# Holding back one weight load until a DMA transpose has landed: part one of the second fc1 block, after layer norm 2's transpose of token tile 1

## The chip, the cores and the metric

The kernel runs on 1 core of one Trainium2 chip. The metric is device time in microseconds (us). Runs are compared only with runs of the same state; where an execution was slow (over 1.5% above the fastest of the same kernel; all others count as fast) or at a lower clock, the text says so. The granted clock is the share of its full speed that TensorE was given. "Issue to landing" runs from the start of a DMA's issue until its data is reported to have arrived. "TensorE" is the matmul engine (PE in the profile; PEld is its weight load), "VectorE" is DVE, "ScalarE" is ACT, "GpSimd" is POOL, and "SyncE" is SP, which here only issues DMAs.

## The reference, cut to what matters

A diffusion-transformer block with B, N, D = 2, 256, 1152 and F = 4608, all in bf16. The part that matters here is the end of the attention half and the start of the MLP half:

```python
x = x + gate_a * (attention(...) @ wo)          # output projection
h2 = _layernorm(x) * (1 + scale_m) + shift_m    # layer norm 2 and its modulate
m = _gelu(h2 @ w_fc1) @ w_fc2                   # fc1: 1152 -> 4608, fc2 back
return x + gate_m * m
```

The 512 tokens are four tiles of 128. Tiles 0 and 1 are batch 0, tiles 2 and 3 are batch 1.

## The kernel before

All weight loads are issued in program order from SyncE. The one that is changed is the first part of the second fc1 block:

```python
    w_shift_m = load_rows("w_shift_m", wmod_v, S_SHIFT_M * D)     # each: 3 loads of 864 KB
    tc.add_manual_dep(first_load["w_shift_m"], transposed.ins.name, WAIT_FOR, ...)
    w_scale_m = load_rows("w_scale_m", wmod_v, S_SCALE_M * D)
    w_f1[0] = load_rows("w_f1_0", wfc1_v, 0)                      # fc1 columns 0 to 1151
    w_f1[1] = wide_tile("w_f1_1")                                 # fc1 columns 1152 to 2303
    for c0, c1 in ((0, PW), (PW, D)):                             # 864 KB, then 1728 KB; PW = 384
        load = nc.sync.dma_start(w_f1[1][:, :, c0:c1], wfc1_v[:, :, D + c0:D + c1])
    w_f1_1_rest = load.ins
    w_f1[2] = load_rows("w_f1_2", wfc1_v, 2 * D)
    # ... further loads
```

Layer norm 2 works by token tile. Each normalized tile is turned by a DMA transpose, issued from ScalarE, into `hT`, which fc1 reads:

```python
    def ln2_normalize(t, split, between):
        # ... rstd; xn2 = (x1 - mean) * rstd, on ScalarE and for odd t partly on VectorE
        nc.scalar.dma_start_transpose(hT[:, :, t * P:(t + 1) * P], xn2[:])

    def wo_group(t, i, pool_add):                 # output projection, 9 matmuls of 384 columns
        for k in range(KD):
            nc.tensor.matmul(pacc[:], aT[:, k, t * P:(t + 1) * P], w_o[:, k, c0:c1],
                             start=(k == 0), stop=(k == KD - 1))
        # ... tmp = pacc * gate_a;  x1 = tmp + x
```

fc1 starts with 12 column tiles (m) for batch 0 alone, then the same 12 for batch 1. Tiles 0 to 8 are in the first block, tiles 9 to 11 in the part that is moved. The second part waits for batch 1's modulate:

```python
    for b in range(B):
        # m = 0..5 stepped over k together, then m = 6..11 one after the other
        # ... f1_mm(..., m, k, b * N, (b + 1) * N, ...): 108 matmuls of 256 columns per batch
        if b == 0:
            mods = [ln2_modulate(1, k) for k in range(KD)]        # VectorE, needs tiles 2 and 3
            tc.add_manual_dep(w_f1_1_rest, mods[0].ins.name, WAIT_FOR, reason="transposes first")
    # ... m = 12..35 over all 512 tokens
```

Of the kernel before, what the change touches and what calls it, by code (L numbers as in the profile page):

```python
# [19 lines left out]
def kernel(  # L20
# [11 lines left out]
    nc = tc.nc  # L32
    B, N, D = x.shape
# [3 lines left out]
    P = 128  # L37
    T = B * N
    NT = T // P
    TPB = N // P  # L40
    KD = D // P
    KF = F // P
    PW = 384
# [6 lines left out]
    WAIT_FOR = mybir.DependencyInfo(mybir.DependencyClass.Sync, mybir.DependencyReason.DATA)  # L50
# [9 lines left out]
    def acc_tile(shape, name, dt=FP32):  # L60
        return psum.tile(shape, dt, name=name, tag="acc", bufs=6)
# [11 lines left out]
    wfc1_v = w_fc1.rearrange("(k p) n -> p k n", p=P)  # L73
# [4 lines left out]
    def wide_tile(name):  # L78
        return wide.tile([P, KD, D], BF16, name=name, tag="wide")
# [37 lines left out]
    def load_rows(name, view, col0):  # L117
        w = wide_tile(name)
        for r in range(0, KD, 3):
            load = nc.sync.dma_start(w[:, r:r + 3, :], view[:, r:r + 3, col0:col0 + D])  # L120
            first_load.setdefault(name, load.ins)
        return w
# [15 lines left out]
    w_f1 = [None] * 4  # L138
# [89 lines left out]
    def ln_exp_rsqrt(dst, var):  # L228
        nc.scalar.activation(dst, var, ACT.Ln, bias=eps_t[:], scale=1.0)
        nc.scalar.activation(dst, dst, ACT.Exp, scale=-0.5)  # L230
# [195 lines left out]
    hT = act.tile([P, KD, T], BF16, name="hT")  # L426
# [189 lines left out]
    w_scale_m = load_rows("w_scale_m", wmod_v, S_SCALE_M * D)  # L616
    w_f1[0] = load_rows("w_f1_0", wfc1_v, 0)
    w_f1[1] = wide_tile("w_f1_1")
    for c0, c1 in ((0, PW), (PW, D)):
        load = nc.sync.dma_start(w_f1[1][:, :, c0:c1], wfc1_v[:, :, D + c0:D + c1])  # L620
    w_f1_1_rest = load.ins
    w_f1[2] = load_rows("w_f1_2", wfc1_v, 2 * D)
    w_f1[3] = load_rows("w_f1_3", wfc1_v, 3 * D)
    w_gate_m = load_rows("w_gate_m", wmod_v, S_GATE_M * D)
# [31 lines left out]
    def ln2_modulate(b, k, eng="d"):  # L656
        h = hT[:, k, b * N:(b + 1) * N]
        if eng == "a":
            return nc.scalar.activation(
                h, h, ACT.Identity, bias=shift_m[:, k, b:b + 1], scale=scale_m[:, k, b:b + 1],  # L660
            )
        return nc.vector.tensor_scalar(
            h, h, scale_m[:, k, b:b + 1], shift_m[:, k, b:b + 1], op0=ALU.mult, op1=ALU.add,
        )

    def ln2_normalize(t, split, between):
        rstd = small.tile([P, 1], FP32, name="rstd", tag="rstd")
        ln_exp_rsqrt(rstd[:], mv2[:, t, 1:2])
        for k, eng in between:
            ln2_modulate(0, k, eng)  # L670
        nb = small.tile([P, 1], FP32, name="nb", tag="nb")
        nc.vector.tensor_scalar(nb[:], mv2[:, t, 0:1], rstd[:], -1.0, op0=ALU.mult, op1=ALU.mult)
        xn2 = work.tile([P, D], BF16, name="xn", tag="xn", bufs=4)
        cs = 5 * P if split else D
        if cs < D:
            nc.vector.tensor_scalar(
                xn2[:, cs:D], x1[:, t, cs:D], mv2[:, t, 0:1], rstd[:],
                op0=ALU.subtract, op1=ALU.mult,
            )
        nc.scalar.activation(xn2[:, 0:cs], x1[:, t, 0:cs], ACT.Identity, bias=nb[:], scale=rstd[:])  # L680
        nc.scalar.dma_start_transpose(hT[:, :, t * P:(t + 1) * P], xn2[:])

    stats2 = [small.tile([P, NPD, 6], FP32, name="stats2", tag="stats2") for _ in range(NT)]

# [18 lines left out]
    def ln2_stats(t, i):  # L703
        nc.vector.bn_stats(stats2[t][:, i, :], x1[:, t, i * PW:(i + 1) * PW])
        if i == NPD - 1:
            nc.vector.bn_aggr(mv2[:, t, :], stats2[t][:].rearrange("p a b -> p (a b)"))
            ln2_normalize(t, t % 2 == 1, BETWEEN.get(t, ()))
# [33 lines left out]
    def f1_mm(dst, m, k, c0, c1, start, **kw):  # L741
        ml = m % KD
        nc.tensor.matmul(  # L743
            dst, w_f1[m // KD][:, k, ml * P:(ml + 1) * P], hT[:, k, c0:c1],
            start=start, stop=(k == KD - 1), **kw,
        )
# [6 lines left out]
    for b in range(B):  # L753
        for stepped in (True, False):
            ms = range(0, MSPLIT // 2) if stepped else range(MSPLIT // 2, MSPLIT)
            accs = {m0: acc_tile([P, 2, N], "pacc") for m0 in ms[::2]} if stepped else {}
            steps = [(m, k) for k in range(KD) for m in ms] if stepped else [(m, k) for m in ms for k in range(KD)]
            for m, k in steps:
                m0 = m - m % 2
                if m0 not in accs:  # L760
                    accs[m0] = acc_tile([P, 2, N], "pacc")
                f1_mm(accs[m0][:, m - m0, :], m, k, b * N, (b + 1) * N, start=(k == 0 and m == m0), skip_group_check=True)
                if k == KD - 1 and m == m0 + 1:
                    nc.scalar.activation(  # L764
                        gT[:, m0:m0 + 2, b * N:(b + 1) * N], accs[m0][:], ACT.Gelu_apprx_tanh,
                    )
        if b == 0:
            mods = [ln2_modulate(1, k) for k in range(KD)]
            tc.add_manual_dep(w_f1_1_rest, mods[0].ins.name, WAIT_FOR, reason="transposes first")
    gate_m = None  # L770
    for m in range(MSPLIT, KF):
        pacc = acc_tile([P, T], "pacc")
# [81 lines left out]
```

## Time and profile before

| | before |
|---|---|
| time, median of 3 | 243.78 us (243.64 to 244.18) |
| span, mean granted TensorE clock | 241.8 us, 0.998 |
| TensorE busy | 235.4 us, 97% |
| the load to be moved: issued, issue to landing | 78.1 us, 17.0 us |
| transposes of tiles 0, 1, 3: issue to landing | 8.4, 3.2, 3.2 us (tile 2's landing is not in this profile) |

The page of the kernel before: the first lines give the span and each engine's busy time; the last is the chain of work that ended last, by engine.

```profile
span 241.8 us, 3979 instructions
PE 235.4 (97%) x1688; PEld 144.4 (60%) x1698; DVE 91.5 (38%) x193; ACT 59.9 (25%) x121; POOL 28.3 (12%) x47
...
PE 94%; issue 2%; ACT 2%; POOL 1%; DVE 0%; POOLq 0%; DVEq 0%; ACTq 0%
```

The same chain in order of time (start us, length us, what), at the place where the output projection (L690) gives way to fc1 (L743). TensorE goes from one to the other without a wait.

```profile
88.90 8.88 PE pacc L690 x54
97.78 23.80 PE pacc L743 x217
```

The timeline around that place (start us, length us, engine, line, operation; in brackets the idle time just before and what ended it). A line ending in "q" is the issuing of a DMA, not its transfer.

```profile
78.09 29.66 SPq L620 DMA_DIRECT2D w_f<-in_w_fc_dram  x2
...
87.33 1.45 ACTq L681 DMA_TRANSPOSE hT<-xn  x1
...
93.66 1.31 ACTq L681 DMA_TRANSPOSE hT<-xn  x1
...
96.48 0.24 DVE L706 BATCH_NORM_AGGREGATE mv<-stats 128x2 f32<-128x18 f32 x1
96.98 0.60 DVE L662 TENSOR_SCALAR hT<-hT,scale_m,shift_m 128x256 bf16<-128x256 bf16 x2 [0.26 <-DMA hT<-xn]
...
97.62 27.63 PE L743 MATMUL pacc<-hT,w_f 128*128 128x256 bf16 x233
...
107.00 2.40 DVE L662 TENSOR_SCALAR hT<-hT,scale_m,shift_m 128x256 bf16<-128x256 bf16 x9 [3.90 <-DMA hT<-xn]
```

The first modulate (L662) is ready 0.26 us after VectorE is, and the first fc1 matmul has no idle in front of it. The bracket on the last line is VectorE waiting for tile 3; TensorE does not wait there.

Issue to landing of the transposes (their line):

```profile
L681 ACTq DMA_TRANSPOSE hT<-xn x4: 1306/1382/1498, 87.3 to 103.7; - x4
DMA to landing us min/median/max: 3.2/3.2/8.4
```

The slow one is tile 0's: in a window that holds only its issue at 87.3 us the same view gives 8.4.

What SyncE's queue waits for (us in total, times, longest). The two parts share line L620.

```profile
SPq L620 <- DVE hT L662: 21.2, 1, 21.2
...
SPq L620 <- DMA w_f<-in_w_fc_dram: 7.9, 1, 7.9
```

### The profile page before, as it was taken

What the parts mean: (1) busy time and instruction counts of PE and PEld (TensorE: products, weight loads), DVE (VectorE), ACT (ScalarE), POOL (GpSimd) and SP (SyncE); (2) the same over time, 40 slices, a digit from 0 to 9 for tenths busy, and PEclk for the clock granted to TensorE, in tenths of its full rate; (3) what the DMA queues carried; (4) which work ended last, traced back from release to release, by engine and by line L of the source; (5) the groups of instructions that cost most, each with busy time, mean ns of one, the idle gap of its engine ahead of it and who ended that gap; (6) DMA issues with size and microseconds to landing.
All of it is one profiled execution on the core that took longest, in us unless ns stands there. A gap on an engine that the chain in (4) does not pass through costs nothing.

```text
span 241.8 us, 3979 instructions
## 1 busy us (share of the span) xinstructions
PE 235.4 (97%) x1688; PEld 144.4 (60%) x1698; DVE 91.5 (38%) x193; ACT 59.9 (25%) x121; POOL 28.3 (12%) x47
## 2 busy tenths in 40 slices
PE   8799999999999999999999999999999999999994
PEld 5585444465567566888844444444556665566674
DVE  3742442319325678830002999960010000000001
ACT  6633322307215032671422333222000000000000
POOL 2300000002300324100000000001121111111111
PEclk9999999999999999999999999999999999999999
DMA  6999999997579999239999999999200000000000
GB/s 188 327 317 310 378 366 393 389 391 247 147 263 398 387 377 159 49 59 361 391 391 391 340 327 284 274 327 284 98 16 16 20 16 16 19 18 19 27 23 16
DMA packets 48781, 53.29 MB, mean 220 GB/s; under 512 B 9587, under 2 KB 36475, under 8 KB 48763
## 3 DMA queue, kind: packets, MB, share of 16 engines
q1 hardware_dynamic: 41312, 50.14, 62.5%
q10 hardware_dynamic: 6939, 1.71, 4.7%
q0 software_dynamic: 512, 1.19, 1.5%
q8 instruction: 13, 0.21, 0.4%
q14 instruction: 5, 0.04, 0.0%
HBM read 50.14 MB, written 1.19 MB: 212 GB/s over the span
## 4 chain that ended last, share of the span: by engine, by line
PE 94%; issue 2%; ACT 2%; POOL 1%; DVE 0%; POOLq 0%; DVEq 0%; ACTq 0%
PE pacc L799 29%; PE pacc L743 29%; PE pacc L690 7%; PE pacc L599 7%; PE pq L521 7%; PE pk L280 5%; PE pk L309 2%; PE pa L639 2%; PE ps_s L556 2%; PE pn L416 2%; ACT sink L206 1%; PE pt L264 1%; PE pm L247 1%; PE pg L498 0%; ACT rstd L335 0%
## 5 line engine op out<-in xcount | busy, mean ns | idle before, releaser
L743 PE MATMUL pacc<-hT,w_f 128*128 128x256 bf16 (+1 forms) x427 | 70.3, 325 | 0.3
L799 PE MATMUL pacc<-w_f,gT 128*128 128x384 bf16 (+2 forms) x468 | 70.5, 314 | 0.0
L799 PEld LDWEIGHTS <-gT 128*128 128x128 bf16 x468 | 44.4, 98 | 26.2
L743 PEld LDWEIGHTS <-w_f 128*128 128x128 bf16 x432 | 42.2, 98 | 27.6
L805 DVE TENSOR_TENSOR tmp<-pacc,gate 128x384 f32<-128x384 f32 (+2 forms) x13 | 6.9, 527 | 65.6 <-PE pacc L799 57.2
L775 ACT ACTIVATE gT<-pacc 128x512 bf16<-128x512 f32 x24 | 14.3, 597 | 32.6 <-PE pacc L743 32.6
L469 DVE SCALAR_TENSOR_TENSOR part<-w_gate_m,s,part 128x1152 f32<-128x1152 bf16 x16 | 21.4, 1414 | 0.0
L807 POOL TENSOR_TENSOR o_sb<-tmp,x 128x384 bf16<-128x384 f32 (+1 forms) x12 | 11.7, 973 | 54.0 <-DVE tmp L805 54.0
L690 PE MATMUL pacc<-w_o,big 128*128 128x384 bf16 x108 | 17.9, 326 | 0.0
L521 PE MATMUL pq<-hT,w_q 128*128 128x512 bf16 x79 | 17.7, 379 | 0.1
L599 PE MATMUL pacc<-w_v,hT 128*128 128x384 bf16 x108 | 17.7, 326 | 0.0
L599 PEld LDWEIGHTS <-hT 128*128 128x128 bf16 x108 | 10.5, 98 | 7.1 <-issue 0.3
L690 PEld LDWEIGHTS <-big 128*128 128x128 bf16 x108 | 10.4, 98 | 7.2 <-issue 0.4
L521 PEld LDWEIGHTS <-w_q 128*128 128x128 bf16 x81 | 7.9, 98 | 9.4
L280 PE MATMUL pk<-big,w_k 128*128 128x256 bf16 (+1 forms) x70 | 13.1, 324 | 0.1
L696 POOL TENSOR_TENSOR x<-tmp,x_sb 128x384 f32<-128x384 f32 x8 | 7.3, 914 | 27.4 <-DVE tmp L695 27.4
L467 DVE TENSOR_SCALAR part<-w_gate_m,s 128x1152 f32<-128x1152 bf16 x2 | 1.6, 818 | 22.3 <-DMA w_gate_m<-in_w_mod_dram 22.3
L491 POOL DMA_DIRECT2D gates_dram<-nat_v x2 | 1.1, 536 | 67.7 <-DVE nat_v L489 67.7
L280 PEld LDWEIGHTS <-w_k 128*128 128x128 bf16 x72 | 6.7, 97 | 3.7 <-issue 0.3
L764 ACT ACTIVATE gT<-pacc 128x512 bf16<-128x512 f32 x12 | 6.5, 598 | 8.9 <-PE pacc L743 8.9
L512 POOL DMA_DIRECT2D gates_dram<-nat x4 | 2.3, 584 | 49.3 <-DVE nat L509 48.7
L695 DVE TENSOR_TENSOR tmp<-pacc,gate 128x384 f32<-128x384 f32 x12 | 6.6, 549 | 3.1 <-PE pacc L690 3.1
(102 smaller groups left out, 164.2 us busy)
## 6 DMA issues: line engine op xcount, KB each, us to landing
w_f<-in_w_fc_dram SPq DMA_DIRECT2D x12, 864.0 KB, 14.9
w_f<-in_w_fc_dram SPq DMA_DIRECT2D x3, 1728.0 KB, 7.9
w_f<-in_w_fc_dram SPq DMA_DIRECT2D x2, 2592.0 KB, 17.2
w_gate_a<-in_w_mod_dram SPq DMA_DIRECT2D x3, 864.0 KB, 11.9
w_v<-in_wqkv_dram SPq DMA_DIRECT2D x3, 864.0 KB, 13.8
w_o<-in_wo_dram SPq DMA_DIRECT2D x3, 864.0 KB, 14.0
w_shift_m<-in_w_mod_dram SPq DMA_DIRECT2D x3, 864.0 KB, 6.6
w_scale_m<-in_w_mod_dram SPq DMA_DIRECT2D x3, 864.0 KB, 12.1
```

The costliest lines, as they stand in the source:

```text
L280: nc.tensor.matmul(pk[m][:, c0:c1], w_k[:, k, m * P:(m + 1) * P], hT0[:, k, c0:c1], start=(k == 0 and c0 == 0), stop=(k == KD - 1), skip_g ...
L469: nc.vector.scalar_tensor_tensor(part[:, b, :], wg[:, k, :], s32[:, k, b:b + 1], part[:, b, :], op0=ALU.mult, op1=ALU.add,)
L521: nc.tensor.matmul(pq[m][:], w_q[:, k, m * P:(m + 1) * P], hT[:, k, :], start=(k == 0), stop=(k == KD - 1), skip_group_check=True,)
L599: nc.tensor.matmul(pacc[:], hT[:, k, t * P:(t + 1) * P], w_v[:, k, pnl * PW:(pnl + 1) * PW], start=(k == 0), stop=(k == KD - 1),)
L690: nc.tensor.matmul(pacc[:], aT[:, k, t * P:(t + 1) * P], w_o[:, k, c0:c1], start=(k == 0), stop=(k == KD - 1),)
L695: nc.vector.tensor_tensor(tmp[:], pacc[:], gate_a[:, b, c0:c1], op=ALU.mult)
L696: (nc.gpsimd if pool_add else nc.vector).tensor_tensor(x1[:, t, c0:c1], tmp[:], x_sb[:, t, c0:c1], op=ALU.add)
L743: nc.tensor.matmul(dst, w_f1[m // KD][:, k, ml * P:(ml + 1) * P], hT[:, k, c0:c1], start=start, stop=(k == KD - 1), **kw,)
L775: nc.scalar.activation(gT[:, m, :], pacc[:], ACT.Gelu_apprx_tanh)
L799: nc.tensor.matmul(pacc[:], gT[:, kk, t * P:(t + 1) * P], w_f2[j][:, r, c0 - n * PW:c0 - n * PW + cw], start=(kk == 0), stop=(kk == KF - 1),)
L805: nc.vector.tensor_tensor(tmp[:], pacc[:], gate_m[:, b, c0:c0 + cw], op=ALU.mult)
L807: (nc.vector if last else nc.gpsimd).tensor_tensor(o_sb[:], tmp[:], x1[:, t, c0:c0 + cw], op=ALU.add)
```

## The change

The intent is to keep the queue free for the transposes: before, 864 KB of weights that nobody needs yet stand in front of them. The order of instructions stays the same on every engine; one wait is added.

```diff
-    for c0, c1 in ((0, PW), (PW, D)):
-        load = nc.sync.dma_start(w_f1[1][:, :, c0:c1], wfc1_v[:, :, D + c0:D + c1])
-    w_f1_1_rest = load.ins
+    w_f1_1_parts = [
+        nc.sync.dma_start(w_f1[1][:, :, c0:c1], wfc1_v[:, :, D + c0:D + c1]).ins
+        for c0, c1 in ((0, PW), (PW, D))
+    ]
@@ ln2_normalize
-        nc.scalar.dma_start_transpose(hT[:, :, t * P:(t + 1) * P], xn2[:])
+        turned = nc.scalar.dma_start_transpose(hT[:, :, t * P:(t + 1) * P], xn2[:])
+        if t == TPB - 1:
+            tc.add_manual_dep(w_f1_1_parts[0], turned.ins.name, WAIT_FOR, reason="transposes first")
@@ after fc1's batch 0
-            tc.add_manual_dep(w_f1_1_rest, mods[0].ins.name, WAIT_FOR, reason="transposes first")
+            tc.add_manual_dep(w_f1_1_parts[1], mods[0].ins.name, WAIT_FOR, reason="transposes first")
```

TPB is 2, so the wait is on token tile 1.

## The prediction

> **What bounds the kernel.** TensorE. The head of the page gives it busy 235.4 of 241.8 us (97%); the chain of waits runs through it for 94%; granted clock 1.00. Where the change acts there is nothing to win back: in windows from 86 to 109 us TensorE is busy in all 23 of 23 us. In the timeline the last output-projection matmul ends at 97.78 us, the first fc1 matmul (L743) starts at 97.62, and the next 132 follow at 110 ns each without a gap.
>
> **What the change does.** No instruction is added, removed or reordered on any engine; only one wait differs. The 864 KB load of the first 384 columns of the second fc1 block, issued at 78.09 us and landing 17 us later (95.1) behind queued loads, is now issued after token tile 1's transpose has landed.
>
> *Gain.* The transposes are issued from ScalarE, the loads from SyncE; the Trainium skill, "DMA: Bandwidth & Descriptors", section "Issuing engines are not separate DMA queues", says that both run on the same 16 engines and interleave. The trace agrees: tile 0's transpose, issued at 87.33 us into a full queue, took 8.4 us to land (95.7), the other three 3.2. Without the 864 KB the weight stream ends about 2.5 us earlier (estimate: 0.88 MB at the 320 to 330 GB/s of 90 to 92 us), so tile 0 lands near 91 to 93.
>
> *Why it is worth nothing.* Batch 0's modulate (VectorE, L662) needs tile 1 too, which is issued at 93.66 us, when the loads are nearly done, and lands at 96.86. VectorE ends its statistics at 96.72 and starts the modulate at 96.98, idle 0.26 us. The first fc1 matmul can then start at 97.3; TensorE is free at 97.6. Gain on the critical path: 0, at most 0.1 us.
>
> *Cost.* The load starts at about 96.9 us. The 1728 KB part of that block took 7.1 us to land with a free queue; half should take about 5 (estimate), landing near 102. Its first reader is column tile 9 in batch 0, the 82nd fc1 matmul: 97.62 + 81 x 0.110 = 106.5 us. Slack 4.5 us. It may delay tile 2's transpose (issued 100.02) by up to 1.5 us, but batch 1's modulate waits for tile 3 (issued 103.69, landed 106.9), when the load is over; TensorE needs batch 1 only at 109.5 us. The second part still waits for that modulate (issued 107.4), so later loads keep their times. Cost 0.
>
> **Predicted time:** 243.8 us, 8 in 10 from 243.3 to 244.4; faster by over 2%: 0.01, within 2%: 0.98, slower by over 2%: 0.01.
>
> **What the profile should show.**
> 1. DMA issues: the slowest of the four transposes falls from 8.4 us to 3 to 6; the others stay at 3.2 (tile 2 perhaps 4 to 5).
> 2. SyncE's waits: a new one on the transpose, some 19 us (78 to 97); the wait on the modulate falls from 21.2 to about 10.
> 3. The first part lands in about 5 us instead of 17.
> 4. The hole in DMA traffic at 97 to 100 us fills; 89 to 92 us empties.
> 5. First fc1 matmul at 97.6 (±0.2), TensorE busy throughout 95 to 115, span 241.8 ± 0.4; the second modulate wait ends at 107.0 ± 0.3.
>
> **What would make it wrong.** The load, meeting the transposes, lands after 106.5 us (TensorE stalls before column tile 9), or delays tile 3's transpose by over 2 us (a stall at batch 1's first matmul). If tile 1's 3.2 us still contain contention, the modulate starts earlier, but TensorE's own work ends at 97.78 and caps the gain.

## The result, and the profile after

| | before | after |
|---|---|---|
| time, median of 6 runs each | 243.65 us (243.57 to 244.18) | 243.47 us (243.17 to 244.06) |
| span, clock | 241.8 us, 0.998 | 241.4 us, 1.000 |
| tile 0's transpose, issue to landing | 8.4 us | 5.1 us |
| the moved load, issue to landing | 17.0 us (from 78.1) | 5.0 us (from 96.5) |
| start of fc1 on the chain, to the end of the span | 97.78, 144.0 us | 97.40, 144.0 us |

The ratio is 0.999, with a 95% interval of 0.9975 to 1.0006: the same time. Here and below a ratio is the mean time of one kernel's fast runs over that of the other's of the same rounds, so it is not quite the ratio of the medians that are quoted.

The lines that answer to those of before. Line numbers have moved: the transposes are L682, the output projection L693, the modulate L663, fc1 L746; the load is still L620. The page of the kernel after:

```profile
span 241.4 us, 3978 instructions
PE 236.4 (98%) x1688; PEld 145.1 (60%) x1698; DVE 91.4 (38%) x193; ACT 59.9 (25%) x121; POOL 28.3 (12%) x47
...
PE 94%; issue 2%; ACT 2%; POOL 1%; DVE 0%; POOLq 0%; DVEq 0%; ACTq 0%
```

Its chain in order of time at the same place:

```profile
88.52 8.88 PE pacc L693 x54
97.40 23.80 PE pacc L746 x217
```

Its timeline:

```profile
86.95 1.26 ACTq L682 DMA_TRANSPOSE hT<-xn  x1
...
93.28 1.31 ACTq L682 DMA_TRANSPOSE hT<-xn  x1
...
96.09 0.24 DVE L709 BATCH_NORM_AGGREGATE mv<-stats 128x2 f32<-128x18 f32 x1
96.54 10.80 SPq L620 DMA_DIRECT2D w_f<-in_w_fc_dram  x2
96.59 0.60 DVE L663 TENSOR_SCALAR hT<-hT,scale_m,shift_m 128x256 bf16<-128x256 bf16 x2 [0.26 <-DMA hT<-xn]
...
97.23 28.06 PE L746 MATMUL pacc<-hT,w_f 128*128 128x256 bf16 x235
...
106.60 2.40 DVE L663 TENSOR_SCALAR hT<-hT,scale_m,shift_m 128x256 bf16<-128x256 bf16 x9 [3.89 <-DMA hT<-xn]
```

Its transposes, from issue to landing (without tile 2's landing):

```profile
L682 ACTq DMA_TRANSPOSE hT<-xn x4: 1259/1310/1335, 86.9 to 103.3; - x4
DMA to landing us min/median/max: 3.2/3.2/5.1
```

What its SyncE queue waits for:

```profile
SPq L620 <- DMA hT<-xn: 18.9, 1, 18.9
...
SPq L620 <- DVE hT L663: 10.2, 1, 10.2
```

The load was moved as intended, by 18 us, and tile 0's transpose lands 3.3 us sooner. Nothing on TensorE answers. VectorE waits the same 0.26 us for the batch 0 modulate. The 0.38 to 0.40 us by which the lines of TensorE, VectorE and ScalarE are earlier here is not due to the change: it is there already before 14 us in the chains (the same group of four x transposes starts at 13.38 us before and at 13.00 after). From the start of fc1 to the end both take 144.0 us.

### The profile page after: what moved, and what is told of

Its sections match the earlier page's. It is cut to its first block, busy times and chain, and to the rows that moved or that the text cites. A ratio compares the mean times of both kernels' runs of the same rounds, so it can differ in the third digit from the quotient of the medians.

```text
span 241.4 us, 3978 instructions
## 1 busy us (share of the span) xinstructions
PE 236.4 (98%) x1688; PEld 145.1 (60%) x1698; DVE 91.4 (38%) x193; ACT 59.9 (25%) x121; POOL 28.3 (12%) x47
## 4 chain that ended last, share of the span: by engine, by line
PE 94%; issue 2%; ACT 2%; POOL 1%; DVE 0%; POOLq 0%; DVEq 0%; ACTq 0%
PE pacc L802 29%; PE pacc L746 29%; PE pacc L693 7%; PE pacc L599 7%; PE pq L521 7%; PE pk L280 5%; PE pk L309 2%; PE pa L640 2%; PE ps_s L556 2%; PE pn L416 2%; ACT sink L206 1%; PE pt L264 1%; PE pm L247 1%; PE pg L498 0%; ACT rstd L335 0%
## 5 line engine op out<-in xcount | busy, mean ns | idle before, releaser
L746 PE MATMUL pacc<-hT,w_f 128*128 128x256 bf16 (+1 forms) x427 | 70.3, 325 | 0.3
L746 PEld LDWEIGHTS <-w_f 128*128 128x128 bf16 x432 | 42.2, 98 | 27.6
L693 PE MATMUL pacc<-w_o,big 128*128 128x384 bf16 x108 | 17.9, 326 | 0.0
L693 PEld LDWEIGHTS <-big 128*128 128x128 bf16 x108 | 10.4, 98 | 7.2 <-issue 0.4
L173 PE MATMUL pwarm<-zeros 128*128 128x256 f32 x18 | 7.4, 587 | 1.2 <-DVE eps_t L93 1.2
```

The source lines that it names most:

```text
L173: nc.tensor.matmul(dst[:, 0:T // 2], zeros32[:, 0:P], zeros32, start=True, stop=True)
L746: nc.tensor.matmul(dst, w_f1[m // KD][:, k, ml * P:(ml + 1) * P], hT[:, k, c0:c1], start=start, stop=(k == KD - 1), **kw,)
```

## The experiments

**Theory A (slack at both ends).** Batch 0's modulate needs tile 1 as well as tile 0, and tile 1 is issued so late that it lands in 3.2 us with or without the load in front. TensorE is also busy with the output projection until just then. At the other end the load has some 4 us to spare before column tile 9 reads it. **Rival B (cancelling).** The earlier tile 0 is a real small gain, which the later load pays back. **Rival C.** Loads and transposes in one another's way cost nothing here, wherever the load stands.

The times of "before" below are those of the kernel before in the same rounds (11 runs per call; median 243.94 in the first call, 243.96 in the second, 243.87 in the third).

### Both kernels again

No edit.

> The kernel before, unchanged, for a second profile of it. All theories: about 243.6 us. Asked of it: whether the landing of token tile 0's transpose (8.4 us in the first profile) and the start of the weight stream (the shift_m load at 67.1 us, 64.8 in the profile after) repeat. If 8.4 comes back near 8, the fall to 5.1 us is due to the change; if it comes back near 5 to 6, part of the fall is the start of the stream, which differs from run to run.

> The changed kernel, unchanged, timed in five rounds. Theory A (slack at both ends: the batch 0 modulate waits for tile 1, which lands fast in both kernels, and the load has some 4 us to spare): ratio 1.000, within 0.998 to 1.002. Rival B (a small gain from the earlier tile 0, paid back by the later load): also near 1, but then fc1 must start earlier against the end of the output projection and stall later, before column tile 9; A expects neither. Tile 0's transpose lands in about 5 us again, tiles 1 to 3 in 3.2.

> The changed kernel once more. One of its 12 timed executions so far took 245.71 us at a mean clock of 0.993, while 28 executions of the kernel before lay between 243.35 and 244.39. If the change brings such executions now and then (TensorE idling before fc1 and falling to half clock, as in the run with the wait on tile 0), about one in ten should show again; if it was a disturbance of that execution, all six should lie between 243.1 and 244.4 and the ratio at 0.998 to 1.001.

Measured. The kernel before, second profile (one run, so of unknown state): 243.39 us, tile 0 lands in 8.7 us, the moved load in 17.3. The kernel after, five rounds: median 243.49 us, ratio 0.9998 (0.9969 to 1.0026); tile 0 lands in 4.7, tile 1 in 3.2, the load in 4.8. Once more: median 243.78 us, ratio 0.9987 (0.9956 to 1.0018); tile 0 in 4.9, tile 1 in 3.2, the load in 5.0. From the start of fc1 on the chain to the end of the span all three take 144.0 us.

The stream of weights starts at different moments from run to run (the shift_m load was issued at 67.1 us in both profiles of before, at 64.8, 65.1 and 68.0 in those of after), but tile 0 took 4.7 to 5.1 in all three, so its fall from 8.4 or 8.7 belongs to the change.

One execution of the changed kernel took 245.71 us at a clock of 0.993. None of the next six did, and one of the 11 executions of the kernel before took 246.33 us at 0.993. Both kernels have such an execution now and then. A mean clock of 0.993 is what the profiles below show where TensorE ran at half clock for one spell of about 3.4 us (1.7 us of clock missing of some 247); no profile caught such an execution of these two kernels, so what sets it off in them is not shown.

### The load after tile 0 instead of tile 1

Against the kernel after:

```diff
-        if t == TPB - 1:
+        if t == 0:
```

> The load now waits for tile 0's transpose instead of tile 1's, so it is issued at about 92 us and its bytes meet tile 1's transpose (issued 93.3). Theory A has only 0.3 us of slack at the modulate, so whatever tile 1 loses goes straight into the time: if transposes wait until queued loads have drained (as tile 0's packets seem to in the traces), tile 1 starts near 96 and lands near 98.5, fc1 starts about 2 us late, 245.5 us (244.5 to 246). If the two queues share the DMA engines evenly, tile 1 loses about 0.6 to 1 us: 244.3. Rival C (contention of loads and transposes costs nothing wherever the load stands): 243.5, tile 1 lands in 3.2 us.

> The kernel with the wait on tile 0 once more: its executions lay between 243.27 and 248.15 us, and the profiled one was a slow one (tile 0 landed at 93.5 us, so the load was issued at the same moment as tile 1's transpose, which then took 6.0 us). Theory A with a race: where tile 0 lands in about 5 us, the load gets in front by 1 us or more and tile 1 lands late by 2 to 4 us (245 to 248 us, with or without half clock); where tile 1's transpose is issued first, it lands in 3.2 us and the time is 243.3. The spread should come back.

Measured. First: ratio 1.0029 (0.9995 to 1.0063); the four fast runs 243.27, 244.24, 245.23 and 246.10 us, two slow runs 247.71 and 248.15. Second: ratio 1.0034 (0.999 to 1.0078), median 244.83 us, all four runs fast (244.78 to 245.34). The second profile, a fast one, its timeline:

```profile
92.30 16.83 SPq L620 DMA_DIRECT2D w_f<-in_w_fc_dram  x2
...
93.67 2.00 ACTq L682 DMA_TRANSPOSE hT<-xn  x1
...
98.43 0.60 DVE L663 TENSOR_SCALAR hT<-hT,scale_m,shift_m 128x256 bf16<-128x256 bf16 x2 [1.70 <-DMA hT<-xn]
98.83 26.55 PE L746 MATMUL pacc<-hT,w_f 128*128 128x256 bf16 x228 [1.03 <-DVE hT L663]
```

The load is issued 1.4 us before tile 1's transpose, which now lands in 4.7 us instead of 3.2. The modulate starts 1.4 us late, and 1.0 us of this reaches TensorE as idle time. By medians the kernel is 0.96 us slower than before (244.83 against 243.87). The intervals of both ratios still include 1, so it is the trace, more than the time, that speaks against Rival C here; the run with more load, below, settles it. There are only 0.3 to 0.4 us of slack.

The first set's profile was of a slow execution (247.71 us), so its time is not compared, but its trace shows a worse meeting. The load was issued at 93.58 us, just after tile 1's transpose at 93.53, which still took 6.0 us to land; after TensorE's idle time the granted clock (third number from the end of the second line) is halved:

```profile
100.06 25.19 PE L746 MATMUL pacc<-hT,w_f 128*128 128x256 bf16 x214 [2.42 <-DVE hT L663]
...
101.00:102.00 1.00, 1.00 (x7) 0.71 (x5) 1.00 (x3) 1.00 (x2) 0.85 (x1) 0.50 0.00 0
```

The spread of the first set (its fast runs reach from no loss to over 2 us) did not come back within the second, where it had been expected to.

### The load after tile 2

Against the kernel after:

```diff
-        if t == TPB - 1:
+        if t == 2:
```

> The load waits for tile 2's transpose: issued at about 102.9 us (99.6 + 3.2), landing 5 us later at 107.9. Theory A puts the first reader, the 82nd fc1 matmul, at 106.3 us, so TensorE stalls about 1.6 us there, once, and the time is 245.1 us (244.4 to 246.0); nothing else moves. Rival C and a load that is not read so early: 243.5 us.

Measured: the four fast runs 246.51 to 249.45 us, ratio 1.0157 (1.0122 to 1.0192), and two slow runs of 250.4 and 250.6 us at a clock of 0.986. In the profile (span 245.4 us, fast) the load was issued at 103.7 us; the chain of work shows how long it took (start us, length us, what):

```profile
103.74 6.30 DMA w_f<-in_w_fc_dram
```

TensorE's timeline:

```profile
98.05 9.01 PE L746 MATMUL pacc<-hT,w_f 128*128 128x256 bf16 x81
110.09 15.13 PE L746 MATMUL pacc<-hT,w_f 128*128 128x256 bf16 x136 [3.03 <-DMA w_f<-in_w_fc_dram]
```

TensorE stops after exactly 81 fc1 matmuls, before column tile 9, as Theory A has it. The stall is 3.03 us, not 1.6. Most of the difference is the landing: the load met tile 3's transpose (issued 104.12) and took 1.3 us longer than the 5.0 us assumed, and that transpose took 6.6 us itself. The slack of the changed kernel is real but small: by the ratio, one token tile later costs 3.8 us. The stall is 3.03 us of it in the profile, whose clock was full; two of the four fast runs also had a lower clock (0.992 and 0.993).

### More load in front of the transposes, without and with the wait

Here the collision is made three times as large. Against the kernel before, the second part loses its wait (the next block takes it over):

```diff
-            tc.add_manual_dep(w_f1_1_rest, mods[0].ins.name, WAIT_FOR, reason="transposes first")
+            tc.add_manual_dep(first_load["w_f1_2"], mods[0].ins.name, WAIT_FOR, reason="transposes first")
```

> The kernel before, with the second part of the block (1728 KB) freed of its wait as well, so that both parts (2.65 MB) stand in the queue in front of the transposes of tiles 0 and 1; the next block's first load takes over the wait for batch 1's modulate, so later loads keep their place. Theory A: the queue drains some 4.5 us later than before (estimate from 1728 KB at about 390 GB/s), near 96, and tiles 0 and 1 land near 100 in place of 96.9; fc1 starts 3 us late and the time is 247 us (246 to 249; TensorE's idle can bring a spell at half clock, as in the run with the wait on tile 0). Rival C (contention costs nothing wherever it stands): 243.6.

Measured: 251.44 us median (250.45 to 253.56), ratio 1.0327 (1.0295 to 1.036). Tile 0's transpose took 13.5 us and landed at 101.0; tile 1's came last, 8.57 us after its issue. The chain and TensorE's timeline:

```profile
93.84 8.57 DMA hT<-xn
...
102.83 22.35 PE L743 MATMUL pacc<-hT,w_f 128*128 128x256 bf16 x188 [4.87 <-DVE hT L662]
```

The stall is 4.87 us, where 3 was expected, and after it the clock falls. The same run in windows of 1 or 2 us (window, its length, then busy us and number of instructions on PE, PEld, DVE, ACT, POOL; then the granted clock, the DMA share and GB/s):

```profile
102.00:103.00 1.00, 0.17 (x2) 0.25 (x3) 0.57 (x3) 0.57 (x2) 0.00 (x0) 1.00 0.00 0
103.00:104.00 1.00, 1.00 (x8) 0.76 (x7) 1.00 (x4) 1.00 (x4) 0.30 (x1) 0.62 0.00 0
104.00:106.00 2.00, 2.00 (x11) 1.45 (x10) 1.97 (x5) 1.25 (x2) 0.61 (x1) 0.50 0.00 0
106.00:108.00 2.00, 2.00 (x18) 1.64 (x16) 1.56 (x7) 1.10 (x3) 0.00 (x0) 0.84 0.79 147
108.00:110.00 2.00, 2.00 (x21) 1.79 (x19) 0.48 (x2) 0.92 (x1) 0.00 (x0) 1.00 0.00 0
```

After the stall TensorE does 11 matmuls in 2 us instead of 21, at a granted clock of 0.50. The Trainium skill, "TensorE: Matmul & The Clock Gate", Part 1, describes this: after an idle window of about 3.4 us the clock is halved until TensorE has again been busy for such a window. The trace agrees in size: 0.38 + 1.0 + 0.32 us of clock are missing in these windows, half of 3.4 us. The stall of 4.87 us and these 1.7 us make up the 6.5 us by which the profiled execution (250.45 us, clock 0.993) is longer than before. It was the fastest of the six; the other five had a clock of 0.984 to 0.986, as if they had about two such spells, but none of these was profiled.

Now with the changed kernel's wait on tile 1 for both parts. Against the kernel after:

```diff
-            tc.add_manual_dep(w_f1_1_parts[1], mods[0].ins.name, WAIT_FOR, reason="transposes first")
+            tc.add_manual_dep(first_load["w_f1_2"], mods[0].ins.name, WAIT_FOR, reason="transposes first")
```

The second part stands behind the first on SyncE's queue, so it waits for tile 1 too.

> The change's wait on tile 1's transpose for both parts, the counterpart of the run before. Theory A: tiles 0 and 1 land as in the changed kernel, fc1 starts on time; the two parts are moved at about 98 to 104.5 us and meet the transposes of tiles 2 and 3, which may make batch 1's modulate 1 to 1.5 us late, within its 2 us of slack. 243.6 us (243.2 to 244.6): the same wait is worth about 3 us here, because here it takes away a collision that reached tile 1.

Measured: 244.87 us median (244.50 to 245.20), ratio 1.0043 (1.0026 to 1.0059). So here the wait is worth 6.6 us (251.44 to 244.87), the lost clock included. It is 0.9 us slower than before, not equal to it, and TensorE's timeline shows where:

```profile
110.57 14.77 PE L746 MATMUL pacc<-hT,w_f 128*128 128x256 bf16 x121 [0.87 <-DVE hT L663]
```

Batch 1's modulate started at 110.16 us instead of 106.6. Tile 2's transpose (issued 99.84) took 9.2 us to land and tile 3's (issued 103.99) took 6.1. What the queues moved in stretches of 2 us (queue 1 carries SyncE's loads, queue 10 ScalarE's DMAs, here only the transposes; packets, MB, share of the 16 engines), at 100 to 102 us, 102 to 104 us and 104 to 106 us:

```profile
q1 hardware_dynamic: 701, 0.72, 109.2%
...
q1 hardware_dynamic: 487, 0.75, 106.5%
...
q1 hardware_dynamic: 407, 0.62, 84.9%
q10 hardware_dynamic: 424, 0.11, 24.2%
```

From 100 to 104 us queue 10 moved nothing, although tile 2's transpose had been handed over by 101.6 us. It gets going only after 104 us, and then the two queues move about as many packets each (407 and 424). A packet of the load is about 1.5 KB there and one of the transpose about 0.25 KB, so equal turns leave the transpose 0.11 MB of 0.73. The same shows in the run before, which had no wait, from 94 to 96 us:

```profile
q1 hardware_dynamic: 417, 0.62, 85.0%
q10 hardware_dynamic: 427, 0.11, 26.1%
```

### TensorE's own work as the only cap?

The prediction gave two reasons for a gain of 0: tile 1's landing and TensorE's own work. Here the second is taken away: six matmuls of the output projection are left out, in both kernels. Their outputs are wrong, which doesn't matter for the times.

```diff
-        for k in range(KD):
+        kd = KD - 2 if t == NT - 1 else KD
+        for k in range(kd):
...
-                start=(k == 0), stop=(k == KD - 1),
+                start=(k == 0), stop=(k == kd - 1),
```

> Wrong result on purpose: the kernel before with 6 of the output projection's matmuls of token tile 3 left out, so TensorE is free 0.98 us earlier (6 x 0.164). It asks whether TensorE's own work was the only cap on the gain. Theory A: the modulate still waits for tile 1 at 96.9 us, fc1 starts at about 97.3 instead of 97.6 to 97.8, so only 0.3 to 0.5 of the 0.98 us are won: 243.2 us, and TensorE idles some 0.5 us before fc1.

> Wrong result on purpose: the changed kernel with the same 6 matmuls left out. Theory A: the same time as the run before within 0.2 us (243.2), with the same idle before fc1, since tile 1 lands at the same time in both. Rival B (the earlier tile 0 is a real gain that TensorE's work hid, paid back elsewhere): fc1 starts earlier here than in the run before and the kernel is 0.3 to 0.6 us faster than it.

Measured: before with the cut 243.82 us (ratio to before 1.0001, 0.9981 to 1.0021), after with the cut 243.57 us (0.9993, 0.9976 to 1.0009). TensorE's timeline of the first:

```profile
97.34 27.84 PE L744 MATMUL pacc<-hT,w_f 128*128 128x256 bf16 x235 [0.67 <-DVE hT L662]
```

and of the second:

```profile
97.59 27.71 PE L747 MATMUL pacc<-hT,w_f 128*128 128x256 bf16 x234 [0.55 <-DVE hT L663]
```

With TensorE free 0.98 us earlier, both kernels idle 0.55 to 0.67 us in front of fc1, waiting for the same modulate. Tile 0's transpose took 8.8 us in one and 5.2 in the other; tile 1's took 3.3 and 3.2. The times differ by 0.25 us, less than the spread of either (about 0.6 to 1.2 us). Neither came down to the expected 243.2 us: what the cut itself should win (0.3 to 0.5 us) did not show in the time either. So the earlier tile 0 is worth nothing that shows even when TensorE could use it, and Rival B, which expected 0.3 to 0.6 us and an earlier fc1, gets no support. A gain of 0.1 or 0.2 us is beyond what these rounds resolve.

## Why the prediction was right

**The time** (243.8, range 243.3 to 244.4): measured 243.47 us against 243.65 before, ratio 0.999. No term of the sum was above 0.1 us, and none was found. The number alone says little: a gain of 0.3 us, as Rival B has it, would have fallen into the range as well. What carries the mechanism is the traces and the runs above.

**Gain of 0.** The mechanism held: tile 0 landed in 5.1 us instead of 8.4, at 92.0 us, in the predicted 91 to 93. Both caps held in the traces: VectorE waits for tile 1 for the same 0.26 us, and TensorE goes on to fc1 without a gap. Tile 1 landed in 3.2 us in all profiles of both kernels (3.3 in the second of before). Taking TensorE's cap away changed nothing between the two kernels. That the collision can cost time at all was shown by the runs that push it onto tile 1: about 1 us with the load after tile 0 (a stall of 1.03 us in the trace), 7.5 us with 2.65 MB in front (in its profile a stall of 4.87 us and 1.7 us of lost clock).

**Cost of 0.** The load landed in 5.0 us, at 101.5, and the first reader was the 82nd fc1 matmul: with the load after tile 2, TensorE stopped after exactly 81. At the pace of the chain, that reader comes at 97.4 + 81 x 0.110 = 106.3 us, so the slack was about 4.8 us against the 4.5 predicted. Tile 2's landing was recorded in neither profile (the "other three" of the prediction are two), so its delay, for which "up to 1.5" had been allowed, is not measured; tile 3 landed in 3.2 us, and batch 1's modulate waited for it as long as before (3.89 and 3.90 us).

**What the profile should show.** Points 1 to 4 came true: the slowest transpose, the waits on SyncE (18.9 and 10.2 us, against 19 and 10), the landing of 5 us, and the hole in DMA traffic at 97 to 100 us, which now carries 50, 280 and 358 GB/s; 89 to 92 us emptied for the loads and kept the rest of tile 0's transpose. Point 5 was right in what it was about, but its absolute times (97.6 and 107.0) came out 0.4 us early (97.23 and 106.60), because that execution started 0.38 us earlier. A time in a trace should be predicted relative to something before the change, such as the end of the output projection.

**What was too small.** Not the prediction, but three expectations took the meeting of loads and transposes too lightly: the stall after tile 2 (3.03 us, not 1.6), the freed second part (4.87 us, not 3, plus the halved clock), and both parts after tile 1 (0.9 us slower, not equal). In the last two, where both queues moved data, they moved equal numbers of packets and not of bytes, and the transpose has the small packets; before that, its queue moved nothing for a while (above). In the changed kernel the load had landed at 101.5 us, before tile 3's transpose was issued (103.30), and batch 1's modulate starts no later for it; so the prediction was not hurt.

## What to carry to other kernels

A long wait in a trace is worth something only if it is the last of the waits that its reader needs: tile 0's 8.4 us looked costly, but the modulate also needs tile 1, which was issued 6 us later and landed in its shortest time anyway. Before moving a load, write down the slack at both ends (here about 0.3 us on the side of the transposes and 4.8 us on the side of the load): one token tile earlier let TensorE idle for 1 us in the fast profile, and one later cost 3.8 us. The same wait that was worth nothing with 0.88 MB in front was worth 6.6 us with 2.65 MB in front, so in this kernel it guards against more load in front even though it does not speed it up.

## What the Trainium skill lacked or had wrong

- "DMA: Bandwidth & Descriptors", sections "Queues, rings and completion order" and "Issuing engines are not separate DMA queues": they say that each engine goes round-robin, packet by packet, between the queues that have work, and that DMAs of different issuing engines interleave. The traces agree once both queues move data (in packets as the profile counts them, 407 beside 424 in the run with both parts after tile 1, 417 beside 427 in the run without the wait). What the page lacks is the time before that: in the run with both parts after tile 1 the transposes' queue moved nothing from 100 to 104 us beside a load stream that had been issued earlier, and tile 2's transpose landed after 9.2 us (3.2 in the run with the load after tile 2, where nothing was in its way). Whether the engines or the making of descriptors holds it back, no run here shows.
- No page has the time from issue to landing of a single DMA transpose of this size from SBUF to SBUF; it would belong to "DMA: Bandwidth & Descriptors". Here one of 128 x 1152 bf16 took 3.2 us with no other traffic (tile 1 in the changed kernel).
- "TensorE: Matmul & The Clock Gate", "Why this matters for your kernels", asks for no idle gaps above about 3 us. In the profiled slow run with the load after tile 0, a gap of 2.42 us was followed by a granted clock of 0.50; in the profiled run with the load after tile 2, a gap of 3.03 us was not. So in these two profiles the length of the gap alone did not decide, and a gap shorter than the figure was not safe.
